# A delta-rule attention followed by an MLP: Winograd's seven products in another bank order, and the steps of every slot listed anew

## The chip, the cores and the metric

The kernel runs on one core of one Trainium2 chip. The metric is the device time of one execution in microseconds. TensorE is called PE (its weight loads PEld), VectorE DVE, ScalarE ACT, GpSimd POOL, and SP issues most of the DMA transfers.

## The reference

Two stages in fp32. The first is a delta rule over B = 4 batches, H = 8 heads, S = 768 tokens, D = 48; the second a layer normalisation, an MLP of width 384 to 1536 to 384 with a ReLU, and a residual.

```python
k_n = k / (np.linalg.norm(k, axis=-1, keepdims=True) + 1e-06)
for t in range(S):
    y[:, :, t] = np.einsum('bhd,bhde->bhe', q[:, :, t], state)
    v_old = np.einsum('bhde,bhd->bhe', state, kt)
    state = state + bt[:, :, :, None] * np.einsum('bhd,bhe->bhde', kt, vt - v_old)
x = y.transpose(0, 2, 1, 3).reshape(B, S, H * D)
xn = (x - mu) / np.sqrt(var + 1e-06) * g_ln
out = x + np.maximum(xn @ w_ch1, 0.0) @ w_ch2
```

Here `kt`, `vt` and `bt` are the normalised key, the value and beta of token t.

## The kernel before

The 768 tokens are cut into 12 chunks of 64. A chunk holds 4 x 64 = 256 tokens, in two groups of 128 partitions. Inside a chunk the recurrence becomes matrix work: a Gram matrix of the keys (`gram`, G), the inverse of a triangular matrix made of it, and products with the state. The inverse is made on DVE, row by row, for two chunks at once: a step called r does two rows (lines 539 and 544, a multiplication and a subtraction each), for blocks of 32 rows (`blocks`), 15 such steps and one row more. For chunks 0 to 3 blocks of 16 rows are used (`first_blocks`, `first_join`). `ga` gathers the blocks (a DVE transpose) and, before the change, also takes a square root on ACT; `no` scales the rows; `own` transposes the result back, `xt` spreads it, `xn` transposes it again for the join of half blocks (`join`, J: products p_e and p_z on PE with evictions between).

`recur(c)` is the recurrence of a chunk: KQ multiplies keys and queries by the state (p_k, p_y) and subtracts p_k from v on DVE; U makes p_u, which ACT evicts; S makes p_s and adds it to the state on DVE; PU adds the second half to p_y, and ACT evicts y; L1 and L2 are the statistics and the scaling of the normalisation on DVE; N transposes on PE and ACT evicts. TK, TQ are DVE transposes of loaded keys and queries, PT the query product (p_g) with its masking on DVE (pt). Vk and Vs take the norms of the keys and scale v.

`mlp(c)` is the MLP of a chunk. H is one of 12 hidden steps: three matmuls of 128x256 into p_h, and a ReLU eviction on ACT into h. The second matrix product is split in 2x2 blocks and made with seven products P1 to P7 instead of eight, in Winograd's way: sums S1 to S4 of blocks of h on DVE (line 786), sums t1 to t4 of the weights made once (T, `sum_blocks`), and additions d1 to d7 on DVE that take PSUM results into the output tiles. A product is six matmuls of 128x192. Two PSUM banks serve it: p_a, and p_o with two halves, c and b. The two banks are the same two that p_h uses in turn (`ps_ffn`).

The order of the work has two parts. Up to chunk 1 and the preparation of chunks 2 and 3, a planner with due times (`Plan`) mixes the generators, and a scheduler places them. From chunk 2 on, slot c does the recurrence of chunk c and the MLP of chunk c-1, in an order written out by hand: the strings in `orders`, `even` and `odd`, run by `slot`. `in_this_order` ties the instructions of every engine to that order, so each engine goes through its own list, and what stands behind a waiting instruction waits too. (a2), (b2), (a4), (b4) name the chunk that a step is for; an apostrophe means the pair before. R does all r steps that are left. In the words of the code, a product and its order before are:

```python
"... P1 S1 d1 ... S2 ... P2 d2 S4 P5 d5 ... P6 d6 ... P3 d3 ... P7 d7 ... P4 d4"
"P1": mul("a", a11, w11, True),   "P2": mul("c", a12, w21, True),
"P5": mul("b", s1, t1),           "P6": mul("a", s2, t2),
"P3": mul("b", s4, w22),          "P7": mul("a", s3, t3),
"P4": mul("c", a22, t4, True),
```

Of the kernel before, what the change touches and what calls it, by code (L numbers as in the profile page):

```python
# [8 lines left out]
FP32 = mybir.dt.float32  # L9
# [10 lines left out]
FB = 16  # L20
# [62 lines left out]
def kernel(  # L83
# [421 lines left out]
    def inverse(nb, L, beta_l, gather, scatter):  # L505

        def square(tile_, i):
            n = nb * L * L
            return tile_[:, i * n : (i + 1) * n].rearrange("p (b s t) -> p b s t", b=nb, s=L)

        def diagonal(t):
            return t.rearrange("p b s t -> p b (s t)")[:, :, 0 :: L + 1]

        both = blk.tile([128, BK * BK], FP32, name="xb")
        xb = square(both, 0)
        if L == FB:
            nc.gpsimd.memset(xb, 0.0)
        else:
            nc.scalar.mul(xb, eps[:, :, None, None].to_broadcast([128, nb, L, L]), 0.0)
        gb = square(both, 1) if L == FB else square(blk.tile([128, BK * BK], FP32, name="gb"), 0)  # L520
        gather(gb)
        nrm = blk.tile([128, BK], FP32, name="nrm")[:, 0 : nb * L].rearrange("p (b s) -> p b s", b=nb)
        nc.scalar.sqrt(nrm, diagonal(gb))
        yield
        nc.vector.tensor_scalar_add(nrm, nrm, 1e-6)
        nc.vector.reciprocal(nrm, nrm)
        db = blk.tile([128, BK], FP32, name="db")[:, 0 : nb * L].rearrange("p (b s) -> p b s", b=nb)
        nc.vector.tensor_tensor(out=db, in0=nrm, in1=nrm, op=ALU.mult)
        nc.vector.tensor_tensor(out=db, in0=db, in1=beta_l, op=ALU.mult)
        nc.vector.tensor_tensor(  # L530
            out=gb, in0=gb, in1=db[:, :, None, :].to_broadcast([128, nb, L, L]), op=ALU.mult
        )
        nc.vector.tensor_copy(out=diagonal(xb), in_=db)
        yield
        tmp = blk.tile([128, (BK // 2) ** 2], FP32, name="tmp")
        for j in range(L - 1):
            n, w = j + 1, L - 1 - j
            t = tmp[:, 0 : nb * n * w].rearrange("p (b s t) -> p b s t", b=nb, t=w)
            nc.vector.tensor_tensor(  # L539
                out=t, in0=xb[:, :, 0:n, j : j + 1].to_broadcast([128, nb, n, w]),  # L540
                in1=gb[:, :, j : j + 1, j + 1 : L].to_broadcast([128, nb, n, w]), op=ALU.mult,
            )
            rest = xb[:, :, 0:n, j + 1 : L]
            nc.vector.tensor_tensor(out=rest, in0=rest, in1=t, op=ALU.subtract)  # L544
            if j % 2:
                yield
        yield from scatter(xb)
# [209 lines left out]
    def mlp(c):  # L757

        h, x = new_h(), xs.pop(c)
        os = [work.tile([128, DM], FP32, name="o") for g in range(2)]
        a11, a21, a12, a22 = (h[i][:, :, g * 128 : (g + 1) * 128] for i in range(2) for g in range(2))

        s1, s2, s3, s4 = a21, a11, late_pool[0].tile([128, HF, 128], FP32, name="s3"), a12
        t1, t2, t3, t4 = (sums[n] for n in ("t1", "t2", "t3", "t4"))
        w11, w21, w22 = w2_sb[:, 0:HF, 0:HM], w2_sb[:, HF:, 0:HM], w2_sb[:, HF:, HM:]
        x11, x12, x21, x22 = (x[:, g, n : n + HM] for g in range(2) for n in (0, HM))  # L770
        o11, o12, o21, o22 = (os[g][:, n : n + HM] for g in range(2) for n in (0, HM))
        p = {}

        def mul(n, a, b, first=False):
            if n == "a" and first:
                p["a"] = ps_ffn([128, HM], "p_a")
            if n == "c" and "c" not in p:
                p_cb = ps_ffn([128, DM], "p_o")
                p.update(c=p_cb[:, 0:HM], b=p_cb[:, HM:])
            for f in range(HF):  # L780
                nc.tensor.matmul(  # L781
                    p[n], a[:, f], b[:, f], start=(first and f == 0), stop=(f == HF - 1), skip_group_check=True,
                )

        def add(out_, in0, in1, op=ALU.add):
            nc.vector.tensor_tensor(out=out_, in0=p[in0] if isinstance(in0, str) else in0, in1=in1, op=op)  # L786

        up = hidden(c, h)
        return {
            "H": lambda: next(up),  # L790
            "S3": lambda: add(s3, a11, a21, ALU.subtract),
            "S1": lambda: add(s1, a21, a22),
            "S2": lambda: add(s2, s1, a11, ALU.subtract),
            "S4": lambda: add(s4, a12, s2, ALU.subtract),
            "P1": lambda: mul("a", a11, w11, True),
            "P2": lambda: mul("c", a12, w21, True),
            "P5": lambda: mul("b", s1, t1),
            "P6": lambda: mul("a", s2, t2),
            "P3": lambda: mul("b", s4, w22),
            "P7": lambda: mul("a", s3, t3),  # L800
            "P4": lambda: mul("c", a22, t4, True),
            "d1": lambda: add(o11, "a", x11),
            "d2": lambda: add(o11, "c", o11),
            "d5": lambda: add(o22, "b", x22),
            "d6": lambda: add(o12, "a", x12),
            "d3": lambda: (add(o12, "b", o12), store(c, 0, os[0])),
            "d7": lambda: (add(o22, "a", o22), add(o21, "a", x21)),
            "d4": lambda: (add(o21, "c", o21), store(c, 1, os[1])),
        }


# [7 lines left out]
    with in_this_order(tc) as last:  # L819
# [4 lines left out]
            grams_01.append(gram(c, fine=True, maker=(ps_two, ps_by)[c]))  # L824
            next(grams_01[c])
        inv = first_blocks(two)
        next(inv)
        next(inv)
        load_blocks(q, 0, 1, (nc.scalar,))
        load_kv(0, nc.scalar)  # L830
        for _ in range(3):
# [74 lines left out]
    plan = Plan()  # L906
# [9 lines left out]
    plan.spread(ffn_0, FT // 2, 20, 42)  # L916
    plan.once(10, queries)
    plan.spread(in_turn(*(prep_g(c, True) for c in (2, 3))), 4, 16, 24)
    plan.spread(first_blocks((2, 3)), 4 + FB // 2, 24, 44)
    plan.spread(prep_p(2), 2, 30, 38)  # L920

    def then(c):
# [7 lines left out]
    with behind(tc, after):  # L930
# [4 lines left out]


    orders = {
        2: """H H H KQ H H H T H T H T H T H U H S3 TK(a2) H P1 S1 d1 TK(b2) S2 S P2 d2 S4 PU P5 d5 L1
            G(a2) P6 d6 L2 TQ(b) P3 d3 N G(b2) P7 d7 ga PT(b) P4 d4 no Vk Vs""",
        3: """H r H KQ H r H r H r U TQ(a2) H r H r H r S H r PU H r H S3 H P1 S1 L1 d1 S2 PT(a2) L2  # L940
            P2 d2 S4 r P5 d5 r P6 d6 TK(a4) N r P3 G(a4) d3 TK(b4) r P7 d7 G(b4) P4 d4 R own Vk Vs""",
        4: """H H KQ xt' H xn' H H J' H H J' H U H J' H ga S H no S3 TQ(b) PU r H P1 L1 S1 PT(b) d1 S2
            L2 P2 d2 S4 r P5 d5 r P6 d6 r N P3 d3 r P7 d7 r P4 d4 Vk Vs""",
        5: """H r H KQ H r r H r H R U TQ(a2) H H own TK(a4) H S H H xt S3 PU H xn H L1 P1 S1 PT(a2) d1
            S2 L2 P2 d2 S4 TK(b4) P5 d5 J P6 d6 G(a4) N P3 d3 J G(b4) P7 d7 J P4 d4 Vk Vs""",
    }
    even = """H H ga KQ no H r H r H r U H r H TQ(b) H r S H r H S3 PU r H H L1 P1 S1 PT(b) d1 S2 L2
        P2 d2 S4 P5 d5 r P6 d6 r N P3 d3 r P7 d7 r P4 d4 Vk Vs"""
    odd = """H r H r KQ H r H H R U TQ(a2) H H own TK(a4) H S H H xt S3 PU H xn H L1 P1 S1 PT(a2) d1 S2
        L2 P2 d2 S4 TK(b4) P5 d5 J P6 d6 G(a4) N P3 d3 J G(b4) P7 d7 J P4 d4 Vk Vs"""  # L950

    def slot(c, order):

# [8 lines left out]
        for token in order.split():  # L962
# [9 lines left out]
            elif name == "T":  # L972
                next(running_sums)
            elif name == "R":
                for _ in range(left.get(m, 0)):
                    next(inverses[m])
                left[m] = 0
            elif name in ("ga", "no", "r", "own", "xt"):
                if m in inverses:
                    left[m] -= name == "r"  # L980
                    next(inverses[m])
            elif name in ("xn", "J"):
                if m in joins:
                    next(joins[m])
            elif name == "Vk":
                if c + 1 < NCH:
                    knrm = norms(c + 1)
            elif name == "Vs":
                if c + 1 < NCH:
                    scale_v(c + 1, knrm)  # L990
            elif x < NCH:
                if name == "TK":
                    new_chunk(x)
                    turned(x, 0, True)
                elif name == "TQ":
                    turned(x, 1, True)
                elif name == "G":
                    next(gram(x), None)
                elif name == "PT":
                    product(x)  # L1000
# [5 lines left out]
    with in_this_order(tc):  # L1006
        for c in range(SLAB, NCH):
            slot(c, orders.get(c, odd if c % SLAB else even))
        steps = mlp(NCH - 1)
        for name in "H H H H H H H H H S3 H H H P1 S1 d1 S2 P2 d2 S4 P5 d5 P6 d6 P3 d3 P7 d7 P4 d4".split():  # L1010
            steps[name]()


# [28 lines left out]
```

## Time and profile before

| | |
|---|---|
| time, median of 3 runs | 618.67 us (616.6 to 621.69) |
| span of the profiled execution | 621.3 us |
| PE busy | 535.5 us (86%) |
| PE weight loads busy | 469.3 us (76%) |
| DVE busy | 388.2 us (62%) |
| ACT busy | 172.5 us (28%) |
| bytes moved, mean rate | 34.56 MB, 56 GB/s |
| hidden steps p_h, L728 | 210.0 us on PE |
| products of the seven, L781 | 75.5 + 25.4 + 25.3 + 23.8 + 23.3 us on PE |
| inverse rows, L539 and L544 | 41.9 + 50.1 us on DVE |
| additions of the seven and sums of h, L786 | 31.3 + 11.7 + 11.6 + 10.5 us on DVE, in their largest groups |

Busy time of PE is modelled from pipelined matmuls and overlaps, so the start times of the instructions, and the idle time in front of them, say more than the sum. Slots differ: even slots from 6 on take 39 us, odd ones 44 to 47 because they prepare the Gram matrices and the join of the pair ahead; slots 2 to 5 carry more DVE work, and the first 195 us hold the loads, the conversion of the weights and chunks 0 to 2.

### The profile page before, as it was taken

Reading aid. Unit: us, or ns where it says so; the run is one execution under the profiler, and the core shown is the slowest. Engines: PE = TensorE matmul, PEld = TensorE weight load, DVE = VectorE, ACT = ScalarE, POOL = GpSimd, SP = SyncE. Lnnn points to the kernel's source line nnn. Section 1 sums busy time; section 2 is a strip of 40 time slices with the busy share of each in tenths; the row PEclk is TensorE's granted clock in tenths of the full one; section 3 lists DMA queues with packets and bytes.
Section 4 is the critical chain, followed back from the end, with each engine's and each line's share of the span. In section 5 each row is a group of like instructions: output and inputs, shape, how many; then the busy total and the mean of one; then the engine's idle time right before and its main releaser. Section 6 shows DMA issues by size and latency. Waiting matters only on the chain.

```text
span 621.3 us, 21738 instructions
## 1 busy us (share of the span) xinstructions
PE 535.5 (86%) x9908; PEld 469.3 (76%) x9908; DVE 388.2 (62%) x805; ACT 172.5 (28%) x355; POOL 16.2 (3%) x38
## 2 busy tenths in 40 slices
PE   2046996868999998989968989989989999899997
PEld 2035775547898887879857879888888788898996
DVE  5846888981547997388961888844979623522312
ACT  1223253122224314512204412316322233123120
POOL 5000110000000000000000000000000000000000
PEclk9999989795799999989978999999999999999999
DMA  4816888531034316023230321301303000010101
GB/s 53 197 47 154 180 213 192 73 66 25 11 43 79 53 15 107 12 27 77 34 45 16 67 26 42 63 3 43 64 2 79 2 16 15 2 26 2 25 1 25
DMA packets 158666, 34.56 MB, mean 56 GB/s; under 512 B 153952, under 2 KB 157040, under 8 KB 158576
## 3 DMA queue, kind: packets, MB, share of 16 engines
q1 hardware_dynamic: 144048, 22.28, 22.0%
q0 software_dynamic: 1456, 7.10, 3.4%
q10 hardware_dynamic: 13072, 3.80, 2.7%
q8 instruction: 77, 1.26, 0.8%
q14 instruction: 13, 0.11, 0.1%
HBM read 28.44 MB, written 4.72 MB: 53 GB/s over the span
## 4 chain that ended last, share of the span: by engine, by line
PE 66%; DVE 21%; issue 6%; ACT 3%; SPq 2%; DMA 2%; ACTq 0%; DVEq 0%
PE p_h L728 27%; PE p_o L781 11%; PE p_a L781 10%; DVE xb L544 4%; DVE tmp L539 4%; PE p_e L564 2%; PE p_z L610 2%; PE p_u L647 2%; PE p_g L356 2%; DVE h L786 2%; PE p_k L636 2%; PE p_g L381 2%; PE p_s L659 2%; PE p_y L667 1%; DVE o L786 1%
## 5 line engine op out<-in xcount | busy, mean ns | idle before, releaser
L728 PE MATMUL p_h<-xnt,w_sb 128*128 128x256 f32 x864 | 210.0, 397 | 4.7 <-ACT h L732 2.2
L728 PEld LDWEIGHTS p_h<-xnt,w_sb 128*128 128x128 f32 x864 | 165.1, 197 | 29.4 <-ACT h L732 2.7
L732 ACT ACTIVATE h<-p_h 128x256 f32<-128x256 f32 x144 | 54.9, 383 | 158.7 <-PE p_h L728 151.8
L781 PE MATMUL p_o<-w_sb,h 128*128 128x192 f32 x396 | 75.5, 343 | 18.8 <-DVE o L786 18.8
L781 PEld LDWEIGHTS p_o<-w_sb,h 128*128 128x128 f32 x396 | 67.1, 199 | 22.4 <-DVE o L786 21.7
L544 DVE TENSOR_TENSOR xb<-xb,tmp 128x31 f32<-128x31 f32 (+20 forms) x154 | 50.1, 326 | 5.3
L539 DVE TENSOR_TENSOR tmp<-xb,gb 128x31 f32<-128x31 f32 (+15 forms) x124 | 41.9, 338 | 2.9
L786 DVE TENSOR_TENSOR h<-h 128x768 f32<-128x768 f32 x33 | 31.3, 949 | 17.8 <-ACT h L732 17.7
L356 PE MATMUL p_g<-kt 48*64 48x64 f32 (+2 forms) x1024 | 16.7, 234 | 16.1 <-DVE kt L334 8.4
L786 DVE TENSOR_TENSOR o<-p_o,o 128x192 f32<-128x192 f32 x33 | 11.7, 353 | 29.2 <-PE p_o L781 29.2
L356 PEld LDWEIGHTS p_g<-kt 48*32 48x32 f32 (+1 forms) x1024 | 14.7, 130 | 18.7 <-DVE kt L334 8.6
L695 ACT COPY xnt<-p_n 128x384 f32<-128x384 f32 x24 | 10.5, 481 | 62.4 <-PE p_n L694 62.4
L594 PE MATMUL p_e<-x_n,gsb 32*32 32x16 f32 x512 | 6.6, 192 | 23.1 <-DVE x_n L589 16.2
L781 PE MATMUL p_a<-t,s 128*128 128x192 f32 x132 | 25.3, 343 | 0.5 <-issue 0.5
L781 PE MATMUL p_a<-t,h 128*128 128x192 f32 x132 | 25.4, 346 | 0.0
L577 ACT ACTIVATE es<-p_e 32x512 f32<-32x512 f32 x23 | 13.5, 588 | 40.3 <-PE p_e L564 36.9
L594 PEld LDWEIGHTS p_e<-x_n,gsb 32*32 32x32 f32 x512 | 6.1, 122 | 24.2 <-ACT xt L399 16.4
L786 DVE TENSOR_TENSOR o<-p_a,x_ln 128x192 f32<-128x192 f32 x33 | 11.6, 351 | 19.6 <-PE p_a L781 19.6
L615 DVE COPY xt<-p_z 32x512 f32<-32x512 f32 x12 | 8.1, 678 | 25.1 <-PE p_z L610 25.1
L781 PE MATMUL p_o<-t,h 128*128 128x192 f32 x132 | 23.8, 331 | 0.0
L781 PEld LDWEIGHTS p_a<-t,h 128*128 128x128 f32 x132 | 23.3, 203 | 0.3
L781 PEld LDWEIGHTS p_a<-t,s 128*128 128x128 f32 x132 | 22.5, 198 | 1.1 <-issue 0.8
(117 smaller groups left out, 734.0 us busy)
## 6 DMA issues: line engine op xcount, KB each, us to landing
words<-in_moe_w_ch_dram POOLq DMA_DIRECT2D x9, 768.0 KB, 5.6
out_dram<-o SPq DMA_DIRECT2D x48, 96.0 KB, 2.2
k<-in_k_dram SPq DMA_DIRECT2D x44, 96.0 KB, 3.4
v_raw<-in_v_dram SPq DMA_DIRECT2D x22, 192.0 KB, 4.2
tb<-in_k_dram SPq DMA_DIRECT2D x48, 64.0 KB, 2.8
tb<-in_q_dram SPq DMA_DIRECT2D x44, 64.0 KB
words<-in_moe_w_ch_dram ACTq DMA_DIRECT2D x3, 768.0 KB, 6.4
tb<-in_q_dram SPq DMA_DIRECT2D x44, 32.0 KB, 2.1
```

The costliest lines, as they stand in the source:

```text
L356: nc.tensor.matmul(out_, kt[rows, i, r0 : r0 + (BK if fine else C)], kt[rows, i, r0:C])
L381: nc.tensor.matmul(p_g[half(e ^ hp), hp, j], kt[rows, i], qt[rows, i])
L539: nc.vector.tensor_tensor(out=t, in0=xb[:, :, 0:n, j : j + 1].to_broadcast([128, nb, n, w]), in1=gb[:, :, j : j + 1, j + 1 : L].to_broadca ...
L544: nc.vector.tensor_tensor(out=rest, in0=rest, in1=t, op=ALU.subtract)
L564: nc.tensor.matmul(p_e[r1, h], gsb[r0, h, BK:C], xn[r0, h])
L577: nc.scalar.mul(es[r1], p_e[r1], -1.0)
L594: nc.tensor.matmul(p_e[q, h], gsb[q, h, 0:BK], xn[q, h, 0:FB])
L610: nc.tensor.matmul(p_z[r0, h], es[r1, h], xt[r1, h, BK:C])
L728: nc.tensor.matmul(p_h, w1_sb[:, t, f * 128 : (f + 1) * 128], xnt[:, t], start=(t == 0), stop=(t == KC - 1),)
L732: nc.scalar.activation(h[f // HF][:, f % HF], p_h, ACTF.Relu)
L781: nc.tensor.matmul(p[n], a[:, f], b[:, f], start=(first and f == 0), stop=(f == HF - 1), skip_group_check=True,)
L786: nc.vector.tensor_tensor(out=out_, in0=p[in0] if isinstance(in0, str) else in0, in1=in1, op=op)
```

## The change

The seven products are put in an order in which neighbours use different banks: P1 (a), P2 (c), P6 (a), P5 (b), P7 (a), P3 (b), P4 (a). P4 now accumulates in bank a on top of P1, P6 and P7, so that one addition (of d7) falls away. S1 and S2 get tiles of their own; S3 and S4 overwrite blocks of h that are no longer read. The square root behind `ga` becomes a step of its own, `sq`. All slots' lists are written anew: KQ stands at the head of each, all H steps stand ahead of PU and P1, S1 and S2 follow P1 directly, and the r steps of chunks 2 to 5 are spread otherwise over slots 3, 4 and 5 (`own` of the first pair moves from slot 3 to slot 4, for one).

```diff
@@ inverse
         gather(gb)
+        yield
         nrm = blk.tile([128, BK], FP32, name="nrm")[:, 0 : nb * L].rearrange("p (b s) -> p b s", b=nb)
@@ mlp
-        s1, s2, s3, s4 = a21, a11, late_pool[0].tile([128, HF, 128], FP32, name="s3"), a12
+        s1, s2, s3, s4 = (
+            work.tile([128, HF, 128], FP32, name="s1", bufs=1),
+            late_pool[0].tile([128, HF, 128], FP32, name="s2"), a21, a12,
+        )
...
-            if n == "a" and first:
+            if not p:
                 p["a"] = ps_ffn([128, HM], "p_a")
-            if n == "c" and "c" not in p:
                 p_cb = ps_ffn([128, DM], "p_o")
...
-            "P4": lambda: mul("c", a22, t4, True),
+            "P4": lambda: mul("a", a22, t4),
...
-            "d7": lambda: (add(o22, "a", o22), add(o21, "a", x21)),
-            "d4": lambda: (add(o21, "c", o21), store(c, 1, os[1])),
+            "d7": lambda: add(o22, "a", o22),
+            "d4": lambda: (add(o21, "a", x21), store(c, 1, os[1])),
@@ the prologue and the plan
-        next(inv)
-        next(inv)
+        for _ in range(3):
+            next(inv)
...
-    plan.spread(first_blocks((2, 3)), 4 + FB // 2, 24, 44)
+    plan.spread(first_blocks((2, 3)), 5 + FB // 2, 24, 44)
@@ orders
-        2: """H H H KQ H H H T H T H T H T H U H S3 TK(a2) H P1 S1 d1 TK(b2) S2 S P2 d2 S4 PU P5 d5 L1
-            G(a2) P6 d6 L2 TQ(b) P3 d3 N G(b2) P7 d7 ga PT(b) P4 d4 no Vk Vs""",
-        3: """H r H KQ H r H r H r U TQ(a2) H r H r H r S H r PU H r H S3 H P1 S1 L1 d1 S2 PT(a2) L2
-            P2 d2 S4 r P5 d5 r P6 d6 TK(a4) N r P3 G(a4) d3 TK(b4) r P7 d7 G(b4) P4 d4 R own Vk Vs""",
-        4: """H H KQ xt' H xn' H H J' H H J' H U H J' H ga S H no S3 TQ(b) PU r H P1 L1 S1 PT(b) d1 S2
-            L2 P2 d2 S4 r P5 d5 r P6 d6 r N P3 d3 r P7 d7 r P4 d4 Vk Vs""",
-        5: """H r H KQ H r r H r H R U TQ(a2) H H own TK(a4) H S H H xt S3 PU H xn H L1 P1 S1 PT(a2) d1
-            S2 L2 P2 d2 S4 TK(b4) P5 d5 J P6 d6 G(a4) N P3 d3 J G(b4) P7 d7 J P4 d4 Vk Vs""",
+        2: """KQ H H H H H H T H T H T H T H U H H TK(a2) P1 S1 S2 d1 TK(b2) S P2 d2 S4 PU P6 d6
+            S3 L1 G(a2) P5 d5 L2 TQ(b) P7 d7 N G(b2) P3 d3 ga PT(b) P4 d4 sq no Vk
+            Vs""",
+        3: """KQ H r H r H r H r U TQ(a2) H r H r H r S H r H r H H H PU P1 L1 S1 S2 d1 PT(a2) P2
+            d2 L2 S4 P6 d6 S3 TK(a4) P5 d5 r N r P7 d7 G(a4) TK(b4) P3 d3 r G(b4) P4
+            d4 r Vk Vs""",
+        4: """KQ H H R' own' H H H xt' xn' H H H J' H J' U H J' ga S H TQ(b) H sq no PU P1 L1 S1
+            S2 d1 PT(b) P2 d2 L2 S4 P6 d6 S3 r P5 d5 r N r P7 d7 r P3 d3 r P4 d4 Vk
+            Vs""",
+        5: """KQ H r H r H r H r U r H r H r H r TQ(a2) S H R H H TK(a4) H own H PU P1 L1 S1 S2 d1
+            PT(a2) P2 d2 L2 S4 P6 xt d6 S3 P5 d5 xn N TK(b4) P7 d7 J G(a4) P3 d3 J
+            G(b4) P4 d4 J Vk Vs""",
     }
-    even = """H H ga KQ no H r H r H r U H r H TQ(b) H r S H r H S3 PU r H H L1 P1 S1 PT(b) d1 S2 L2
-        P2 d2 S4 P5 d5 r P6 d6 r N P3 d3 r P7 d7 r P4 d4 Vk Vs"""
-    odd = """H r H r KQ H r H H R U TQ(a2) H H own TK(a4) H S H H xt S3 PU H xn H L1 P1 S1 PT(a2) d1 S2
-        L2 P2 d2 S4 TK(b4) P5 d5 J P6 d6 G(a4) N P3 d3 J G(b4) P7 d7 J P4 d4 Vk Vs"""
+    even = """KQ H ga H H H sq no H r U H r H TQ(b) H r S H r H r H H PU P1 r L1 S1 S2 d1 PT(b) P2
+            d2 L2 S4 P6 d6 S3 r P5 d5 r N P7 d7 r P3 d3 r P4 d4 Vk Vs"""
+    odd = """KQ H r H r H r H H R U TQ(a2) H H own TK(a4) H S H H xt H xn H PU P1 L1 S1 S2 d1
+            PT(a2) P2 d2 L2 S4 P6 d6 S3 TK(b4) J P5 d5 G(a4) N P7 d7 J P3 d3 G(b4) J
+            P4 d4 Vk Vs"""
@@ the tail (the last MLP)
-        for name in "H H H H H H H H H S3 H H H P1 S1 d1 S2 P2 d2 S4 P5 d5 P6 d6 P3 d3 P7 d7 P4 d4".split():
+        for name in "H H H H H H H H H H H H P1 S1 S2 d1 P2 d2 S4 P6 d6 S3 P5 d5 P7 d7 P3 d3 P4 d4".split():
```

More of the change, by code (lines that the diff above doesn't have):

```diff
@@ L977, in slot @@
                 left[m] = 0
-            elif name in ("ga", "no", "r", "own", "xt"):
+            elif name in ("ga", "sq", "no", "r", "own", "xt"):
                 if m in inverses:
```

## The prediction

> **What bounds the kernel now.** I read the page first: TensorE (PE) is busy 86% of the span and VectorE (DVE) 62%. The chain that ended last says the same by line, so the question is where PE stands still, and I asked for PE's own waits and then for the busy times slot by slot.
>
> ```profile
> PE 535.5 (86%) x9908; PEld 469.3 (76%) x9908; DVE 388.2 (62%) x805; ACT 172.5 (28%) x355; POOL 16.2 (3%) x38
> ...
> PE   2046996868999998989968989989989999899997
> ...
> PEclk9999989795799999989978999999999999999999
> ...
> PE 66%; DVE 21%; issue 6%; ACT 3%; SPq 2%; DMA 2%; ACTq 0%; DVEq 0%
> ```
>
> The waits of PE, longest first (total, times, longest):
>
> ```profile
> PE p_o L781 <- DVE o L786: 18.8, 10, 5.9
> ```
>
> One wait stands out: a product into the bank of p_o waits for DVE's addition out of it, ten times, in every slot from 3 on and in the tail. The timeline of slot 8 shows it:
>
> ```profile
> 453.50 1.16 PE L381 MATMUL p_g<-qt,kt 48*64 48x64 f32 x64
> ...
> 454.59 2.22 PE L781 MATMUL p_o<-w_sb,h 128*128 128x192 f32 x12
> 454.73 1.22 DVE L383 TENSOR_TENSOR pt<-p_g,pmask 128x1024 f32<-128x1024 f32 x1 [1.70 <-PE p_g L381]
> 455.87 0.35 DVE L786 TENSOR_TENSOR o<-p_a,x_ln 128x192 f32<-128x192 f32 x1
> 456.14 0.95 DVE L786 TENSOR_TENSOR h<-h 128x768 f32<-128x768 f32 x1
> ...
> 457.98 0.35 DVE L786 TENSOR_TENSOR o<-p_o,o 128x192 f32<-128x192 f32 x1
> ...
> 458.39 1.41 PE L781 MATMUL p_o<-w_sb,h 128*128 128x192 f32 x7 [1.57 <-DVE o L786]
> ```
>
> P2 (454.59) ends near 456.8. P5 goes to the other half of the same bank, so it waits for d2, and d2 stands on DVE behind pt, d1, S2 and the normalisation: 458.33. PE starts 0.06 later. Wait by wait, slots 3 to 11 and the tail lose 1.27, 2.69, 5.90, 1.57, 1.58, 1.58, 1.57, 1.57, 0.61 and 0.45 us: 18.8.
>
> By stage (start:end; length, then PE, PEld, DVE, ACT, POOL busy; then the granted clock): first the joins of chunks 2 and 3, up to slot 2's p_u; then the rest of slot 2; then slots 3 to 6, each from the end of one last product to the next.
>
> ```profile
> 128.90:170.90 42.00, 35.13 (x958) 29.73 (x959) 19.64 (x27) 10.62 (x23) 0.30 (x1) 0.72 0.18 35
> 170.90:195.70 24.80, 24.62 (x488) 22.76 (x488) 13.05 (x22) 9.93 (x18) 0.00 (x0) 1.00 0.36 48
> 195.70:237.30 41.60, 40.15 (x676) 35.73 (x676) 36.58 (x87) 12.55 (x26) 0.00 (x0) 1.00 0.31 53
> 237.30:285.50 48.20, 43.29 (x804) 38.49 (x803) 33.62 (x76) 15.18 (x33) 0.00 (x0) 0.96 0.25 42
> 285.50:344.20 58.70, 50.52 (x931) 44.83 (x931) 36.05 (x76) 16.01 (x32) 0.00 (x0) 0.88 0.27 42
> 344.20:383.30 39.10, 37.53 (x548) 33.74 (x547) 33.37 (x77) 10.97 (x25) 0.00 (x0) 1.00 0.23 42
> ```
>
> The reader is to see that slot 5 takes 58.7 us where slot 7, which issues as many PE instructions, takes 46.7 at full clock, and that the joins run at clock 0.72.
>
> [...] P5 never starts before d2 is done, though their columns differ. [...] after the waits of 2.69 and 5.90 us the records show half clock for 3.4 and 10.2 us, P5 takes 3.83 and 4.21 us instead of 2.22, and after waits of 1.57 nothing slows. [...] what stands behind a waiting product waits too, as the timeline shows.
>
> **The change, part by part.** Prices, all from the trace: a product 1.95 us (2.1 after a change of shape), a hidden step (H) 1.30, KQ 2.05, p_u, p_s and the second half of p_y 1.08 each, the query product 1.1; on DVE a sum over h 0.95, an addition out of PSUM 0.35, pt 1.22, L1 1.5, L2 1.0, an inverse step r of two rows 0.95 to 1.83, own 2.07.
>
> *Bank order.* P1 a, P2 c, P6 a, P5 b, P7 a, P3 b, P4 a: each product now waits for the addition two products back. d4 loses one addition (11 x 0.36 us on DVE, which hides beside PE). S1 and S2 in their own tiles no longer wait for S3 and P1; same size, same 0.95. Walking an even slot from P1's start at 0: PE does P1 to 1.95, PT to 3.05, P2 to 5.15. DVE: y is evicted at 0.9, L1 to 2.4, S1 3.35, S2 4.3, d1 4.6, pt 5.8, d2 6.1, L2 7.1, S4 8.0, d6 8.3, S3 9.2. P6 needs S2 and d1 (4.6): starts at 5.15 without a wait. P5 (7.1) needs d2 (6.1). N, then P7 (9.7) needs S3 (9.2). P3 (11.65) needs d5 (11.3), P4 (13.6) needs d7 (13.4). So slots 6, 8, 10 lose no time, with 0.2 to 0.5 us to spare: -1.57 each; the same walk for 7 and 9: -1.57 each. Sum 7.9. In the tail nothing waits: -0.45. In slot 11, without PT between P1 and P2, P6 comes at 3.9 but d1 at 4.6: about 0.7 lost instead of 0.61, no gain.
>
> *KQ first.* Now H1 needs p_a's bank, which d4 leaves last; d4 ends up to 1.9 us after P4, because an r stands before it. KQ's 2.05 us hide that, barely. The third H still waits for the first one's eviction at the old distance. Cost 0 to 0.5 in all.
>
> *Own step for the square root (sq).* ACT stands in wait for gb 2.7 us in three places; H evictions behind it have slack: 0.
>
> *Slot 2.* The same walk gives 20.6 us from P1 to P4's end, where it takes 21.1 (174.66 to 195.74): -0.5.
>
> *Slot 3.* No wait for d2, but G(b4) needs the second key transpose, which stands on DVE behind d5, two r, d7: ready at 15.9, PE there at 14.7. New wait 1.2; KQ to P4's end 39.8 instead of 41.5: -1.7.
>
> *Slot 4.* Here own moved in from slot 3, so the start wait for H's eviction (2.2) goes; J' stands 0.5 for x_n. p_u now directly follows the second J', and its input is copied out of PSUM by DVE and then ACT (0.68 + 0.58 plus passing on): new wait 1.4. DVE reaches L1 2.4 us after P1's start, so P6 waits 1.05, later ones 0.3. Total 43.6 instead of 48.2: -4.6, with the half-clock stretch gone (1.6 of it).
>
> *Slot 5.* Ten r instead of nine, s_all and a key transpose now stand on DVE ahead of own. From the end of slot 4's P4: scaled v 5.1, eight r 18.8, query transpose 20.0, s_all 20.9, two r 23.3, key transpose 24.5, own 27.0, L1 28.5, S1, S2, d1 30.7. PE reaches P6 at 26.05: a wait of about 4.7 instead of 5.9, again long enough for half clock. After it every addend is on time; with one slow product the slot ends at 49.3. Today's slot also has a stop of 2.07 us inside p_g with no cause in the profile ("issue") and a second half-clock stretch; if such a stop comes back it is 51.5. I take 50.7: -8.
>
> *Joins of chunks 2 and 3 (128.9 to p_u at 170.9).* Until 128.9 the order on every engine is the same. KQ of chunk 2 (2.05 us at full clock, but 1.09 + 1.80 + 1.94 and more in today's half clock) moves to 128.9, where PE now idles 1.95 for L753. Of the ten H steps' 30 matmuls nine stand among the joins and 21 behind them; after, 12 and 18. PE's work here is 22.7 us (KQ 2.05, ten H 13.0, first joins 4.3, joins 3.4) in 42: the rest is half clock (140 to 163.9), four "issue" gaps of 4.8, and the relay between DVE, ACT and PE. The relay, walked at full clock without those gaps, brings p_u to 156.7 (-14); with half clock from about 133 to 150 and the gaps, to about 164 to 167. I take 164: -7, ends -2 and -14.
>
> *Sum:* 7.9 + 0.45 + 0.5 + 1.7 + 4.6 + 8 + 7 - 0.5 = 29.6. 618.67 - 29.6 = 589.1; I say 590.
>
> **Rivals.** A: as above, 590. B: VectorE takes the wait over where it is fullest. Slots 3 to 5 are 88%, 70% and 61% busy on DVE, and its backlog just before P1 is what I find again in slot 5; if slots 3, 4 and 5 together give 3 us, and the joins, bound by their relay, 1, the time is 618.67 - 8.4 - 0.5 - 4 = 606. Against it: in slots 4 and 5 half clock and the start wait alone cost 10 us. C, slower: KQ at the head and the r before d4 make H1 wait for d4. If DVE runs one r (1.75) later than I walked, H1 waits 1.75 in eight slots (14), P6, P7 and P4 in the same slots a further 1.5 (12), slot 5's wait grows to 7, and the joins with KQ and four row sums ahead of x_n lose 3; against 18.8 removed that is about +10: 629. For it: margins of 0.2 to 0.5 us; against it: a late DVE catches up in the H part, where it has 4 us of idle time. D: the wait passes from P5 to P6 or P7 at the same length, and the joins do not move: 618.
>
> **How the numbers follow.** A 0.66, B 0.24, D 0.04, C 0.06. A alone spans 582 to 598 through the joins (-14 to -2) and slot 5 (-5 to -11); B reaches 606, so the range is 580 to 606. Faster by over 1%: A and B, 0.90; within 1%: 0.04; slower: 0.06.
>
> **What would show it.** PE's waits after: the wait of p_o for o, ten times, gone; in its place p_a for o or s in slots 4 (about 1 us), 5 (about 4.7) and 11 (0.7), and p_g for kt in slot 3. Slots 6, 8 and 10 at 37.5 instead of 39.1. p_u of slot 2 at 162 to 167, KQ of slot 2 at 128.9. Slot 5 near 50 with one half-clock stretch after its wait. PE busy time lower only by what half clock added; DVE busy lower by 4. I am wrong if slots 6 to 10 keep 39 us, if H waits for d4, or if the joins' stage stays near 42.

## The result, and the profile after

The changed kernel takes 592.18 us (median of 4 runs, 588.2 to 593.15) where the kernel before takes 620.18 (616.6 to 622.02): ratio 0.9543, 95% interval 0.9477 to 0.9609. The forecast was 590.0, range 580 to 606. The profiled executions are 621.3 and 590.7 us long, 30.6 apart. Further down, medians are of all runs, ratios leave out the runs that lie more than 1.5% above the fastest of their kernel (8 of 18 for z2), and the profiled execution of x1 was disturbed (704.4 us at a granted clock of 0.76), so that its kernel was run again as z1.

The page after, busy times first, then PE's row, its clock, and the engines' shares of the chain that ended last:

```profile
PE 520.6 (88%) x9908; PEld 459.9 (78%) x9908; DVE 384.4 (65%) x794; ACT 173.5 (29%) x355; POOL 16.2 (3%) x38
...
PE   2046797687999999999977999999999999999997
...
PEclk9999999795899999999999899999999999999999
...
PE 71%; DVE 12%; issue 6%; DMA 4%; ACT 4%; SPq 2%; ACTq 1%; POOL 0%; DVEq 0%; POOLq 0%
```

DVE's share of the chain fell from 21% to 12% although DVE is only 3.8 us less busy: what went is not DVE's work but PE's waiting for it. PE itself is 14.9 us less busy, with the same 9908 matmuls; the clock row has one 8 in the right-hand half where before it had a 7 and an 8.

The five longest waits of PE from 150 to 620 us (total, times, longest):

```profile
PE p_a L784 <- DVE o L789: 2.8, 2, 2.4
PE p_y L637 <- issue: 2.0, 1, 2.0
PE p_g L356 <- issue: 1.1, 1, 1.1
PE p_a L784 <- DVE h L789: 1.0, 1, 1.0
PE p_u L648 <- DVE xt L616: 0.8, 1, 0.8
```

The wait of p_o for o (18.8 us, ten times) is not there at all. Of what the forecast put in its place, p_a for o is there twice, 2.43 in slot 5 and 0.40 in slot 11. No hidden step waits for d4. New is the second line, a stop of PE that no semaphore explains.

The timeline of slot 8, the slot shown before:

```profile
429.46 1.16 PE L381 MATMUL p_g<-qt,kt 48*64 48x64 f32 x64
430.55 2.22 PE L784 MATMUL p_o<-w_sb,h 128*128 128x192 f32 x12
431.47 0.35 DVE L789 TENSOR_TENSOR o<-p_a,x_ln 128x192 f32<-128x192 f32 x1
431.74 1.21 DVE L383 TENSOR_TENSOR pt<-p_g,pmask 128x1024 f32<-128x1024 f32 x1
432.61 2.12 PE L784 MATMUL p_a<-t,s 128*128 128x192 f32 x12
432.87 0.35 DVE L789 TENSOR_TENSOR o<-p_o,o 128x192 f32<-128x192 f32 x1
...
434.56 1.63 PE L784 MATMUL p_o<-w_sb,s 128*128 128x192 f32 x9
```

P6 follows P2 after 2.06 us into the other bank, while d2 (432.87) runs beside it; before, P5 followed P2 after 3.80. The difference is 1.74: the wait of 1.57, and the 0.16 us by which two products overlap when nothing stands between them (P2's end is modelled at 432.77, P6 starts at 432.61).

By stage, in the form of the table before: joins, slot 2, then slots 3 to 6 (the end of slot 5 is here the end of its P4):

```profile
126.70:164.60 37.90, 31.76 (x961) 27.23 (x960) 18.87 (x29) 10.62 (x23) 0.30 (x1) 0.73 0.25 45
164.60:189.40 24.80, 24.62 (x487) 22.58 (x486) 13.93 (x22) 10.18 (x18) 0.00 (x0) 1.00 0.28 38
189.40:229.50 40.10, 39.92 (x675) 35.75 (x674) 35.25 (x82) 12.42 (x26) 0.00 (x0) 1.00 0.34 54
229.50:272.40 42.90, 41.64 (x807) 37.26 (x810) 32.57 (x74) 15.52 (x33) 0.00 (x0) 1.00 0.26 44
272.40:320.00 47.60, 43.07 (x878) 38.32 (x880) 37.02 (x80) 14.81 (x29) 0.00 (x0) 1.00 0.35 56
320.00:362.00 42.00, 40.00 (x618) 36.03 (x614) 32.05 (x72) 12.28 (x28) 0.00 (x0) 0.96 0.20 35
```

Slots 4 and 5 now run at clock 1.00 where they had 0.96 and 0.88; the joins still have 0.73; and slot 6 got longer, 42.0 against 39.1, with a piece of half clock.

| stage | before, us | after, us | difference | forecast |
|---|---|---|---|---|
| up to the joins | 128.8 | 126.7 | -2.1 | 0 |
| joins | 42.1 | 37.9 | -4.2 | -7 |
| slot 2 | 24.9 | 24.9 | 0 | -0.5 |
| slot 3 | 41.6 | 40.1 | -1.5 | -1.7 |
| slot 4 | 48.1 | 42.8 | -5.3 | -4.6 |
| slots 5 and 6 | 97.8 | 89.5 | -8.3 | -9.6 |
| slots 7 to 10 | 168.5 | 160.2 | -8.3 | -6.3 |
| slot 11 and tail, to its last product | 65.4 | 64.5 | -0.9 | -0.45 |

The first row is no effect: the trace shows the same order of instructions there in both kernels, and the joins began anywhere from 122.2 to 129.9 us in the kernels below. The last join step of slot 5 (1.1 us of PE) stands behind P4 after, so that slot 6 holds it; the two slots are therefore taken together.

### The profile page after: what moved, and what is told of

Read it like the earlier page. It is cut to its first block, busy times and chain, and to the rows that moved or that the text cites. A ratio compares the mean times of both kernels' runs of the same rounds, so it can differ in the third digit from the quotient of the medians.

```text
span 590.7 us, 21727 instructions
## 1 busy us (share of the span) xinstructions
PE 520.6 (88%) x9908; PEld 459.9 (78%) x9908; DVE 384.4 (65%) x794; ACT 173.5 (29%) x355; POOL 16.2 (3%) x38
## 4 chain that ended last, share of the span: by engine, by line
PE 71%; DVE 12%; issue 6%; DMA 4%; ACT 4%; SPq 2%; ACTq 1%; POOL 0%; DVEq 0%; POOLq 0%
PE p_h L729 30%; PE p_a L784 12%; PE p_o L784 9%; DVE tmp L540 2%; DVE xb L545 2%; PE p_e L565 2%; PE p_z L611 2%; PE p_u L648 2%; PE p_g L356 2%; PE p_g L381 2%; PE p_y L668 2%; PE p_y L637 2%; PE p_s L660 2%; PE p_k L637 1%; PE p_z L603 1%
## 5 line engine op out<-in xcount | busy, mean ns | idle before, releaser
L729 PE MATMUL p_h<-xnt,w_sb 128*128 128x256 f32 x864 | 202.7, 391 | 0.6 <-ACT xnt L696 0.6
L729 PEld LDWEIGHTS p_h<-xnt,w_sb 128*128 128x128 f32 x864 | 164.6, 194 | 24.5 <-ACT xnt L696 1.0
L784 PE MATMUL p_a<-t,h 128*128 128x192 f32 x264 | 47.2, 329 | 1.0 <-DVE h L789 1.0
L784 PE MATMUL p_o<-w_sb,h 128*128 128x192 f32 x264 | 48.0, 332 | 0.0
L784 PEld LDWEIGHTS p_a<-t,h 128*128 128x128 f32 x264 | 42.8, 190 | 1.5 <-DVE h L789 1.3
L784 PEld LDWEIGHTS p_o<-w_sb,h 128*128 128x128 f32 x264 | 42.7, 190 | 0.9
L679 DVE BATCH_NORM_STATS2 st<-x_ln 128x6 f32<-128x384 f32 x24 | 12.9, 541 | 35.6 <-ACT x_ln L673 35.6
L789 DVE TENSOR_TENSOR s<-h 128x768 f32<-128x768 f32 x11 | 10.2, 931 | 25.9 <-ACT h L733 25.9
L784 PE MATMUL p_a<-t,s 128*128 128x192 f32 x132 | 23.6, 329 | 2.8 <-DVE o L789 2.8
L696 ACT COPY xnt<-p_n 128x384 f32<-128x384 f32 x24 | 10.5, 482 | 50.0 <-PE p_n L695 49.9
L784 PE MATMUL p_a<-w_sb,h 128*128 128x192 f32 x132 | 24.2, 334 | 0.0
L784 PE MATMUL p_o<-w_sb,s 128*128 128x192 f32 x132 | 23.6, 329 | 0.0
```

Of the source, the lines that this page charges most:

```text
L679: nc.vector.bn_stats(out=st[:, g], in_=y[:, g])
L729: nc.tensor.matmul(p_h, w1_sb[:, t, f * 128 : (f + 1) * 128], xnt[:, t], start=(t == 0), stop=(t == KC - 1),)
L784: nc.tensor.matmul(p[n], a[:, f], b[:, f], start=(first and f == 0), stop=(f == HF - 1), skip_group_check=True,)
```

## The experiments

**1. The two halves of the change.** Theory: the bank order removes the wait wherever DVE is late, and the lists gain on their own in the joins and in slots 3 to 5. Rival: either half alone does it all, the other being needed for nothing.

z1 (and x1, the same kernel) has the changed products, their banks and the own tiles, but keeps the lists of before: only the product steps are put in their new order, each in about its old place. An even slot, against the kernel before:

```diff
-... L1 P1 S1 PT(b) d1 S2 L2 P2 d2 S4 P5 d5 r P6 d6 r N P3 d3 r P7 d7 r P4 d4 Vk Vs
+... L1 P1 S1 S2 PT(b) d1 L2 P2 d2 S4 P6 d6 S3 r P5 d5 r N P7 d7 r P3 d3 r P4 d4 Vk Vs
```

x2 has the changed lists, but the products, banks and tiles of before. An even slot, against the changed kernel:

```diff
-... H H PU P1 r L1 S1 S2 d1 PT(b) P2 d2 L2 S4 P6 d6 S3 r P5 d5 r N P7 d7 r P3 d3 r P4 d4
+... H H S3 PU P1 r L1 S1 S2 d1 PT(b) P2 d2 L2 S4 P5 d5 r P6 d6 r N P3 d3 r P7 d7 r P4 d4
```

> The kernel before with the products' new bank order and the own tiles of S1 and S2 alone; every list keeps its places for KQ, H, r, own, xt, J, and no step of its own for the square root. Theory 1 (the wait for d2 is most of the gain): the ten waits of a product for the addition out of its own bank go, 18.8 us, and with them the half-clock stretches behind the two long ones; 596 to 602 us, p_u of slot 2 still 42 us after the first MLP's end, the 2.2 us wait of H for its eviction at slot 4's start still there. Theory 2 (the lists are the gain): DVE's backlog in slots 3 to 5 and the place of L1 make P6 wait as long as P5 did; 609 to 616 us.

> The changed kernel's lists (KQ first, H ahead of PU, rows spread otherwise, square root apart) with the seven products in the old order, in the old banks, and S1 and S2 in place. Theory 1: p_o waits for o again, about 1.6 us in slots 6 to 10 and more in 3 to 5; only the joins (4 us), slot 4's start wait (2 us) and some of slot 5 are won: 606 to 613 us. Theory 2: most of the gain is there without the banks: 596 to 602 us. If the two parts simply add, the gains of this run and of the one with the banks alone make 28 us.

> The same kernel as in the run with the banks alone, taken again for a profile that can be read by stage. After that run's time (gain near 15 us) both theories stand on their middle. Theory 1: PE's wait for d2 is gone and no wait of its size took its place: slots 6, 8 and 10 at 37.2 to 37.8 us, slot 5 with 2 to 4 us of wait; joins 42, slot 4 with the start wait of 2.2 us: 600 to 605 us. Theory 2: half of the wait passed on to P6 (d1 stands behind pt and L1): slots 6 to 10 near 38.3 us each.

Measured: x1 604.68 us, 0.9707 (0.9609 to 0.9805); z1 603.70, 0.9762 (0.9715 to 0.9809); x2 606.48, 0.9771 (0.9689 to 0.9853). Against the runs of the kernel before beside them, z1 gains 618.92 - 603.70 = 15.2 us and x2 619.71 - 606.48 = 13.2: together 28.4, where the whole change gains 28.0. Each half does about half, and neither stands in for the other, which neither theory of x1 had: its time lies between their ranges. The own tiles of S1 and S2 belong to z1's half (experiment 5 takes them out alone). The longest waits of PE in z1 from 150 to 620 us:

```profile
PE p_a L783 <- DVE o L788: 4.5, 2, 3.8
PE p_h L728 <- ACT h L732: 2.2, 1, 2.2
PE p_g L356 <- issue: 1.6, 1, 1.6
PE p_g L356 <- DVE kt L334: 0.9, 1, 0.9
```

The banks alone take the wait away in slots 6 to 10 (37.2, 44.6, 37.2, 41.8, 37.2 us long; after, slots 7 to 10 have 44.1, 37.2, 41.8, 37.2) and leave slot 5 at 54.1, where DVE is behind: its P6 waits 3.8 for d1. The wait of slot 4's first hidden steps (2.2) is there too. The same list of x2:

```profile
PE p_o L782 <- DVE o L787: 11.5, 10, 4.3
PE p_y L637 <- issue: 1.9, 1, 1.9
PE p_u L648 <- DVE xt L616: 0.8, 1, 0.8
```

The lists alone keep all ten waits but shorten eight of them: in slot 3 from 1.27 and in slots 6 to 10 from about 1.57 to 0.57. By the lists this is because S1, S2 and d1 stand before pt, and L2 behind d2. The wait of slot 11 grows from 0.61 to 0.93, that of the tail stays at 0.45. So 0.57 us a slot is still the price of the products' old order, banks and tiles. The lists' own gain is the joins (37.9 us) and slots 4 and 5 (45.2 and 49.9 against 48.1 and 58.7); in slot 6 they lose (43.0 against 39.1, of which 1.1 is the join step that moved there).

**2. KQ at the head.** Theory: the joins gain from KQ, which fills a wait of PE, and slot 6 pays for it. Rival: KQ at the head is worth its few microseconds in every slot. x3 moves KQ back in all slots, y1 in all but slot 2, and z2 moves it to the head in slot 2 of the kernel before and does nothing else.

```diff
# x3, an even slot (y1 the same, but slot 2 stays as after)
-KQ H ga H H H sq no H r U
+H ga H KQ H H sq no H r U
# z2, slot 2 of the kernel before
-H H H KQ H H H T H T
+KQ H H H H H H T H T
```

> The changed kernel with KQ back behind as many H steps as before in every slot. Theory 1 (KQ first hides d4 and fills the joins): the joins take 41 to 42 us again (+4), and H waits for d4 up to 0.6 us in the slots where an r stands before d4: 595 to 600 us. Theory 2 (its place matters little): the joins' length is set by the relay between DVE, ACT and PE, and where KQ no longer follows p_z and p_g directly in slot 6, the stop of 2.0 us inside p_y goes, with its half clock: 588 to 592 us.

> The changed kernel with KQ at the head in slot 2 alone; in all other slots it stands behind the H steps again, as before. Theory 1 (KQ first pays in the joins and costs in slot 6[...]): joins 38 us as with KQ first, slot 6 near 38.5 without the stop of 2.0 us in p_y and its half clock: 587 to 590 us, about 4 below the changed kernel. Theory 2 (the stop in slot 6 and the joins' length come and go from run to run): 591 to 594 us. Theory 3 (KQ first hides d4 in all slots): H waits for d4 again: 594 to 597 us.

> The kernel before with one move: KQ at the head of slot 2 instead of behind three H. Theory 1 (the joins' gain is KQ's alone, which fills the wait of PE ahead of them): joins 38 us instead of 42, the rest unchanged: 614 to 617 us. Theory 2 (the rest of the new lists is needed for it, or the wait only moves to x_n): joins 41 to 42, 617 to 621 us.

Measured: x3 592.86 us, 0.9560 (0.9490 to 0.9631); y1 590.24, 0.9513 (0.9470 to 0.9555); z2 615.77, 0.9904 (0.9867 to 0.9940). The times of x3, y1 and after can't be told apart, so the 4 us that y1 was expected to gain over the changed kernel are not shown; the stages can be told apart. The joins take 42.2 us in x3, 38.0 in y1 and 37.9 after. In z2, with KQ at the head of slot 2 alone, they take 38.8, 3.3 less than before; its median is 618.92 - 615.77 = 3.2 us lower, its ratio gives 5.9 (3.7 to 8.2). PE's waits in the joins, first of x3, then of after:

```profile
PE p_h L729 <- DVE o L754: 2.4, 1, 2.4
PE p_e L595 <- issue: 2.0, 1, 2.0
PE p_e L565 <- issue: 1.9, 1, 1.9
PE p_z L603 <- issue: 0.9, 2, 0.5
```

```profile
PE p_e L595 <- DVE x_n L590: 2.8, 1, 2.8
PE p_e L595 <- issue: 1.8, 1, 1.8
PE p_z L603 <- issue: 1.5, 2, 1.0
```

KQ stands where PE waited for L754; the wait then moves on to x_n, 2.8 us, since the first join is there sooner than its input. Over the undisturbed traces, the joins take 42.1 or 42.2 us in the three with KQ further back (before, z1, x3; half clock for 23.9 us in each). With KQ at the head, five take 37.9 to 38.2 (after, x2, y1, y2, y3) and z2 takes 38.8; these six wait 2.0 to 2.8 us for x_n and have half clock for 20.5 us. The other three, z3, x4 and y4, take 40.1, 40.8 and 40.9: they wait 4.1 us for x_n, and x4 and y4 have half clock for 23.9 us again. So KQ at the head is worth between 1.3 and 4.3 us. Why x_n is later in those three is not shown.

In slot 6 it is the other way: 38.5 us in x3 and in y1, 42.0 after. That slot's head after, as the timeline shows it:

```profile
320.92 1.15 PE L637 MATMUL p_k<-s_all,kt 48*64 48x48 f32 x64
...
321.89 0.99 PE L637 MATMUL p_y<-s_all,qt 48*64 48x48 f32 x56
...
324.89 0.47 PE L637 MATMUL p_y<-s_all,qt 48*64 48x48 f32 x8 [2.00 <-issue]
```

KQ stops in its middle for 2.00 us and no semaphore is named; from 324.8 the clock is halved for 3.4 us. Ahead of it stand a last Gram product, P4 and the last join step. With KQ two hidden steps later, as in x3 and y1, the same matmuls run through. One more thing can be read from x3 and y1: no hidden step waits for d4 there either, although H stands directly behind P4.

**3. Is it the run of small matmuls?** y4 moves the last join step of slot 5 ahead of P4, so that P4's large matmuls stand between it and KQ.

```diff
-P3 d3 J G(b4) P4 d4 J Vk Vs
+P3 d3 J G(b4) J P4 d4 Vk Vs
```

> The changed kernel with one move: in slot 5 the last join step (64 matmuls of 32x32) goes ahead of P4 instead of behind it, so that twelve large matmuls stand between it and KQ's 128 small ones. Theory 1[...]: the stop of 2.0 us shrinks to under 0.5 and the half-clock window behind it goes: slots 5 and 6 together 3 to 4 us shorter, 588 to 590 us. Theory 2 (p_y waits for something that the profile does not show, as an eviction from its bank): the stop stays, 591 to 594 us.

Measured: 592.16 us, 0.9554 (0.9499 to 0.9608). The stop is gone and slot 6 takes 37.2 us, 4.8 less than after: 2.0 of stop, about 1.7 of half clock (an estimate, half of 3.4 us), and 1.1 for the join step that is back in slot 5. But the time is that of after, since slot 5 takes 50.7 instead of 47.5: the join step, and half clock from 301.1 and from 318.1, 3.4 us each. So it is shown that slot 6 stops because the join step and KQ stand in a row; a gain by this edit is not shown.

**4. The rows of chunks 2 to 5.** x4 has everything of after except that slots 3 to 5 keep the r steps, own, xt, xn and J nearly where they were before.

```diff
# slot 3, from P6
-P6 d6 S3 TK(a4) P5 d5 r N r P7 d7 G(a4) TK(b4) P3 d3 r G(b4) P4 d4 r Vk Vs
+r P6 d6 S3 TK(a4) r P5 d5 r N P7 d7 G(a4) TK(b4) P3 d3 r G(b4) P4 d4 R own Vk Vs
# slot 4
-KQ H H R' own' H H H xt' xn' H H H J' H J' U H J' ga S
+KQ H H xt' H xn' H H J' H H J' H U H J' H ga S
```

> The changed kernel with the r, R, own, xt, xn and J steps of slots 3 to 5 placed nearly as before (own of the first pair at slot 3's end, r among P2, P6, P5 in slot 3, six r in slot 4, xt and xn ahead of PU in slot 5). Theory 1: about 2 us come back at slot 4's start, where ksum stands behind own, and slot 5's wait before P6 grows from 2.4 to 5 or 6, long enough for half clock: 597 to 602 us. Theory 2: with the banks alternating, where the rows stand matters little, and slot 4's waits (p_u for its copied input) go: 590 to 593 us.

Measured: 597.63 us, 0.9653 (0.9583 to 0.9724), 5.5 us above after, though the intervals overlap. Slots 3 to 5 take 41.2 + 46.3 + 50.9 = 138.4 us where after has 40.1 + 42.8 + 47.5 = 130.4: of these 8.0 us, 2.1 are waits of PE (7.7 us in x4, above all P6's 2.8 in slot 5 and 1.8 of slot 4's hidden steps; 5.6 after), up to 3.4 the 6.8 us of half clock from 313.8 (an estimate, half of them), and 1.1 the last join step, which lies in slot 5 here; some 1.4 stay open. Slot 6 gives 4.1 back: its stop is 0.43 instead of 2.00, without half clock, and the join step is not in it.

**5. Own tiles for S1 and S2.** y3 computes S1 and S2 in place of blocks of h, so that S3 must come first:

```diff
-P1 r L1 S1 S2 d1 PT(b) P2 d2 L2 S4 P6 d6 S3 r P5
+P1 r L1 S3 S1 S2 d1 PT(b) P2 d2 L2 S4 P6 d6 r P5
```

> The changed kernel without the own tiles: S1 and S2 overwrite blocks of h as before, S3 gets its tile and so stands ahead of S1 on DVE, and S2 waits for P1. The bank order and the lists stay. Theory 1 (the own tiles are needed for the margin before P6): d1 comes 0.95 us later, P6 waits 0.3 to 0.5 us in the slots with PT and 1.4 in slot 11, while P7 no longer waits for S3: 594 to 598 us. Theory 2 (a plain swap on DVE, hidden): 591 to 594 us.

Measured: 596.67 us, 0.9611 (0.9549 to 0.9672), 4.5 us above after, with intervals that overlap. PE's p_a waits for o nine times, 6.5 us in all, instead of twice and 2.8; slots 7 to 10 are each 0.4 to 0.5 us longer and slot 11 is 1.0 longer. The sum over h that stands ahead of d1 uses up the margin of P6, which the forecast gave as 0.2 to 0.5.

**6. The step for the square root.** z3 takes the extra step out again (`sq` is part of `ga`).

> The changed kernel without the own step for the square root: it stands behind ga on ACT again. Theory 1 (the evictions of H behind it have slack): 591 to 594 us, no wait of PE for h. Theory 2 (in slots 2, 4, 6 and 8 ACT stands 1 to 2 us for gb, and H for its bank): 594 to 598 us.

Measured: 591.66 us, 0.9579 (0.9529 to 0.9628): no difference from after. One wait of 0.5 us of H for ACT comes back in slot 8 alone (38.0 against 37.2).

**7. A better version.** y2 is y1 with less on DVE ahead of slot 5's P6: own is taken earlier, and the key transpose TK(a4), xt, the Gram product and two join steps later, the last join step behind two hidden steps of slot 6. In slot 4 a hidden step stands between the second join step and U, so that U's input is copied meanwhile.

```diff
# slot 4
-J' H J' U H J' ga S
+J' H J' H U J' ga S
# slot 5
-r TQ(a2) S H R H H TK(a4) H own H PU P1 L1 S1 S2 d1 PT(a2) P2 d2 L2 S4 P6 xt d6 S3 P5 d5 xn N TK(b4) P7 d7 J G(a4) P3 d3 J G(b4) P4 d4 J Vk Vs
+r TQ(a2) S H R H H own H H PU P1 L1 S1 S2 d1 PT(a2) P2 d2 L2 S4 P6 d6 S3 P5 d5 xt N xn P7 P3 d7 TK(a4) J d3 G(a4) TK(b4) P4 d4 J G(b4) Vk Vs
# slot 6
-H ga H KQ H H sq no
+H H J' KQ ga H H sq no
```

> As the run with KQ first in slot 2 alone, and besides: in slot 4 one H between the second join step and U, so that p_u's input is copied meanwhile; in slot 5 own ahead of the key transpose, xt and xn behind d5, P3 ahead of the joins, and the last join step moved into slot 6. If slots 4 and 5 lose what the trace shows (p_u for xt about 1, P6 2.4, P7 1.0, p_g 1.1 us), this is 3 to 5 us below the run with KQ first once: 582 to 587 us. If the waits only pass to the next product, since DVE is late by the same work: 587 to 590 us.

Measured: 585.11 us (584.56 to 586.91), 0.9443 (0.9405 to 0.9480): faster than both kernels. Its slowest run (586.91) lies below the fastest of after (588.2), though the ends of the two intervals meet; against y1 (586.33 to 591.88) the runs just overlap. Its slots 4 to 6:

```profile
229.90:271.40 41.50, 41.49 (x803) 36.97 (x802) 32.68 (x74) 15.21 (x33) 0.00 (x0) 1.00 0.26 46
271.40:312.30 40.90, 39.83 (x679) 35.41 (x678) 36.17 (x78) 10.55 (x23) 0.00 (x0) 1.00 0.28 48
312.30:354.60 42.30, 41.43 (x804) 37.30 (x804) 32.62 (x73) 16.59 (x34) 0.00 (x0) 1.00 0.31 51
```

All three at clock 1.00, and PE idle 2.0 us in 124.7 us; slots 4 to 6 take 132.5 us after. A Gram product and a join step moved from slot 5 to slot 6, so the two are to be read together: 83.2 us, where y1 has 85.6 and after 89.5.

## Why the prediction was right, point by point

**The reason held.** The wait of p_o for o was the loss it was taken for. All ten are gone; slots 8 to 10 became 1.8 to 2.0 us shorter, slot 7 2.7, against 1.57 forecast; part of the rest is the overlap of two products that a wait takes away (1.74 per slot in the timeline). z1 shows that the bank order, with the own tiles, does this without the lists. No run parts the bank from the tile, though: before, both halves are one tile, p_o, and the program's own semaphores for that tile could make P5 wait for d2 as well. What is shown is that of the products which alternate between p_a and p_o none waits for o in slots 6 to 10, neither in z1 nor after, while each of these slots lost 1.57 us before.

**The joins: right direction, mis-sized.** Forecast -7, came -4.2; p_u stood at 164.6, where 164 was forecast, but 2.1 us of that belongs to the stretch ahead. Two terms were mis-sized: half clock, estimated "from about 133 to 150", lasted from 130.2 for 20.5 us instead of 17; and KQ did fill the wait for L753, but PE then waited 2.76 us for x_n, a wait that the forecast did not have.

**Slot 5: more than forecast, by another make-up.** Forecast was -8; its own length fell by 11.2, or 10.1 without what the last join step took along into slot 6 (1.1). Expected were a P6 wait of 4.7, half clock behind it and perhaps a stop of 2. The timeline after:

```profile
296.01 2.12 DVE L463 STREAM_TRANSPOSE own<-xb 128x1024 f32<-128x1024 f32 x1
...
301.18 0.35 DVE L789 TENSOR_TENSOR o<-p_a,x_ln 128x192 f32<-128x192 f32 x1
...
301.59 2.22 PE L784 MATMUL p_a<-t,s 128*128 128x192 f32 x12 [2.43 <-DVE o L789]
...
307.43 2.22 PE L784 MATMUL p_a<-t,h 128*128 128x192 f32 x12 [1.01 <-DVE h L789]
```

From the end of slot 4's P4 (272.4) d1 ended at 29.1, not 30.7, and PE stood at P6 at 26.8, not 26.05: 2.43 in place of 4.7. The term that was mis-sized is the start of DVE's walk: the rows began at 4.1 where the walk said 5.1, and 0.3 us more was saved up to own and 0.3 behind it. No half clock followed in this execution (the stage from 272.4 to 320.0 has clock 1.00); in y4, behind the same wait, it did for 3.4 us, and the last section has what the traces show of the difference. A wait of 1.01 that was not forecast stands at P7, whose sum S3 lies behind xt on DVE.

**Slot 6: the step that failed.** Forecast -1.57, came +2.9, of which 1.1 is the join step. A stop like slot 5's was reckoned with in slot 5, where p_g indeed kept one of 1.08; that KQ at the head would make slot 6 a place for one was missed, 2.00 us of stop and 3.4 us at half clock. What KQ at the head gains in the joins, 1.3 to 4.3, it loses in slot 6: 3.5 against x3 and y1.

**Smaller terms.** Slot 3: -1.5 for -1.7, but G(b4) did not wait for the key transpose, where 1.2 was forecast (its 0.2 is for an ACT copy, gsb). Slot 4: -5.3 for -4.6; p_u waits 0.8 and 0.3 instead of 1.4, P6 not at all instead of 1.05. Slot 2: nothing for -0.5. Slot 11: its P6 waits 0.40, about 0.7 was forecast. DVE busy -3.8 for -4. The square root's own step: nothing, as forecast.

**The rivals.** B (VectorE takes the wait over) is seen only as 2.43 in slot 5; slots 3 to 5 together gave 1.5 + 5.3 + 11.2 = 18.0 us, 16.9 without the join step that moved, not 3. C did not come, and its premise, that H1 needs the bank which d4 leaves last, does not hold: in x3, where H1 stands directly behind P4, it starts before d4 (at the end of slot 6 at 362.73, d4 from 363.39 to 363.74), so it does not write what d4 reads. Only the second H comes after d4, by 0.2 to 0.7 us in x3. KQ at the head was not needed to hide d4. y3 shows how near the rest of C was, P6 waiting for a late DVE: one sum of 0.95 more ahead of d1 costs about 0.5 in most slots. D did not come: P6 and P7 wait in slots 5 and 11 alone.

**The total is nearer than its terms, and that is luck.** Joins and slot 6 gave 2.8 + 4.5 = 7.3 us less than forecast, and the start, slot 4, slot 5 and slots 7 to 10 gave 2.1 + 0.7 + 3.2 + 2.0 = 8.0 more. Errors of both signs cancelled; the 2.1 of the start is no effect of the change at all.

## What to carry to other kernels

Where a tile's results are added out of PSUM by another engine, order the products so that neighbours use different banks and tiles; the reader then has a whole product's time (here 2.06 us from P2 to P6, with the addition of 0.35 beside it). Here ten waits, 18.8 us in all, went, p_a now waits 2.8 us for o and 1.0 for h, and DVE was only 3.8 us less busy. A list written anew should be judged stage by stage against its halves: here one move (KQ at the head) gained up to four microseconds in one stage and lost as much in another. And where DVE is the late one, look for what stands ahead of the one addition that PE waits for, and move that, not the work as a whole.

## What the runs showed of the hardware that was not expected

**Stops of PE at fixed distances.** The stops put down to "issue" stand at the same few matmuls, counted from the start, whatever that matmul is: in the joins at numbers 2391, 2519 and 2647 after (0.42, 1.82 and 1.05 us), and at 2391, 2518 and 2646 before (2.33, 0.67 and 1.40; a record or so is missing), in a p_z here and a p_e there, so 128 matmuls apart; in slots 5 and 6 near 5830 (2.07 before, 1.08 after) and 6085 (2.00 after). Not every trace stops at each of them. (Counted are the trace's records, two for each matmul of the program: 864 for the 432 of the hidden steps.) In the traces of the kernels before and after, the stops of over 0.4 us from the joins on last up to 2.33 us. Ahead of the ones at p_g and p_y after stand 128 small matmuls, which took 1.5 and 2.2 us. The stop at p_y is there in all four traces in which the join step and KQ stand in a row behind P4 (after, x2, y3, z3: 1.72 to 2.00 us); y2, with two hidden steps ahead of that row, has 0.85. With large matmuls among the last 128, which then took 3 to 4.6 us, it is 0.43 in x4 and absent in x3, y1 and y4. Small matmuls alone do not bring it every time: p_g in slot 5 stops for 1.08 after and not at all in y4, behind the same order.

What PE waits for at these places no trace shows. That the stop at p_y is smaller or absent where larger matmuls stand in between is shown by x4, x3, y1 and y4.

**The same wait with and without half clock.** After and y4 have the same order up to slot 5's P6 and the same wait of 2.43 us there. After keeps full clock to the end of the slot; in y4 the records show half clock for 3.4 us from 301.1. Where the half clock starts tells part of the difference. In each of the three traces its stretches start whole multiples of 3.41 us apart: before at 85.4, 109.2, 140.0, 273.1, 317.5 and 337.9 (7, 9, 39, 13 and 6 times 3.41), after at 106.3, 130.2 and 324.8 (7 and 57 times), in y4 at 301.1 and 318.1 (5 times). When the span is cut into pieces of 3.41 us that fit these starts, all 2.43 us of y4 lie in one piece, the one that ends at 301.1; after, 1.74 us fall into one piece and 0.7 into the next. The other pieces at full clock in the traces of before and after, from 190 to 560 us, are in line with that: where no small matmul ran, the two with 2.59 and 3.41 us of idle PE (the waits of 2.69 and 5.90 before) were followed by half clock, and none with 1.82 or less was; where small matmuls ran, the two with 1.79 (before, ahead of 337.9) and 1.90 (after, ahead of 324.8) were, and none with 1.08 or less was.

So the wait of 2.43 us between large matmuls cost its length after, and in y4 also up to half of the 3.4 us at half clock behind it (an estimate; behind the wait of 5.90 before, half clock lasted 10.2 us). That its place made the difference is inferred from these few cases; how the clock is granted is not shown. A single profile does not tell which of the two a change has bought.
